# Chunked attention with a feed-forward block on one core: 64-token chunks as four 64x64 TensorE tiles

## The chip, the cores and the metric

The kernel runs on one NeuronCore of one Trainium2 chip. Five engines work from queues of their own: TensorE (PE, matrix products, with weight loads listed as PEld), VectorE (DVE), ScalarE (ACT), GpSimd (POOL) and SyncE (SP, which issues nearly all the transfers). [...] The metric is the device time of one execution in microseconds (us); lower is better.

## What is computed

Six groups of 512 tokens go through a decayed linear attention with 8 heads of 64 columns, then through an RMS norm and a gated feed-forward block (512 to 1536 to 512). Cut to what matters:

```python
# attention, per batch (4) and head (8), 768 tokens, blocks of 64
Dmask = lam ** (i - j) where i >= j else 0          # 64 x 64
intra = (q_b @ k_b.T * Dmask) @ v_b
inter = (q_b * lam ** (pos + 1)) @ kv_state
out_b = intra + inter
kv_state = lam ** 64 * kv_state + (k_b * lam ** (63 - pos)).T @ v_b
# block, per token
xn = x / sqrt(mean(x * x) + 1e-6) * rms_g
y = (silu(xn @ w_gate) * (xn @ w_val)) @ w_out
```

The block size of the recurrence is free: the same output comes from blocks of 128 with lam ** 128. The products have to be good to float32. The feed-forward splits its operands into a high and a low 16-bit part and adds three products; the attention uses float32 operands as they are.

## The kernel before

**Tiling.** The 3072 tokens are six groups m of 512, each with four chunks of 128 tokens (GC = 4); six chunks make one sequence, after which the state starts again. The 8 heads are four pairs p; a pair fills the 128 partitions, one head in each half. Pair(m, p) is one unit of attention, and there are 24 of them. The feed-forward is cut into 72 units u = (m, f), f being one of 12 blocks of 128 hidden columns. Units of the first 24 places are "classical" (line 761: gate and value products, 128x512); the later ones use a scheme with seven half-size products (line 948). Lines 780 to 782 are the output product.

**One pair of attention** has these steps.

- scores (line 507): keys by queries, 8 matmuls, one for each chunk and head. A head has 64 rows of the array (its partitions) and all 128 columns, so two matmuls, one for each head, can be under way at once. A row of the trace shows this form as 64*128.
- decay_k (ACT, line 517), decay_a (DVE, line 527, from PSUM, 128x512 twice), decay_q (POOL, line 531).
- state_sums (line 540): decayed keys by values, 128 tokens deep, 64x64 out; form 128*64. The last chunk of a sequence needs none, so there are 8 or 6 matmuls.
- states (DVE, lines 553 and 555): the running state, one 64-column operation for each chunk, straight from PSUM.
- mix_chunks (line 572): values by decayed scores, form 128*64, 8 matmuls of 128 columns. mix_states (line 583): state by queries, form 64*64, 8 matmuls or 6 (the first chunk of a sequence has no state), added to the same bank.
- keep_output (ACT, line 595) and keep_squares (ACT, line 606), both from PSUM.

A float32 matmul runs as two passes, so the trace counts 16 where the program has 8.

**Order.** Nothing is scheduled on the chip: each engine runs its instructions in program order. A class Plan takes all steps with an engine, a cost, a due time, what they read and write and which buffers they need, and lists them in the order of a list scheduler; a table SHIFTS moves the due times of single steps. TURN is what it adds when PE goes from one kind of matmul to another. Where it sees PE idle early on, busy() (line 142) puts in matmuls of the identity whose result is not read. The first group's attention and norm run alone (the ramp, until the first row of line 761); the other 19 pairs lie between the products of the feed-forward units.

**Banks.** PSUM has eight banks of 128x512 float32: ps0, ps1 (scores, and the products of even late units), pg, pv (classical products, products of odd late units, and a pair's state sums and output), po0 to po3 (output products).

Of the kernel before, what the change touches and what calls it, by code (L numbers as in the profile page):

```python
# [9 lines left out]
F32 = mybir.dt.float32  # L10
# [7 lines left out]
P = 128  # L18
# [5 lines left out]
def retention_swiglu_kernel(  # L24
# [28 lines left out]
    heads = [slice(j * D, (j + 1) * D) for j in range(2)]  # L53
# [21 lines left out]
    lam_b, lam_p, gcol = cs[:, :H], cs[:, H : H + NP], cs[:, H + NP :]  # L75
# [60 lines left out]
    SLOTS = GC + 1  # L136

    def busy(n, bank=3):

        ps = ps_out.tile([P, DM], F32, tag=f"po{bank}", name=f"unread{bank}")  # L140
        for _ in range(n):
            nc.tensor.matmul(ps[:, :P], ident, ident, start=True, stop=True)

    state = const.tile([P, NP, SLOTS, D], F32, name="state")


    mask = const.tile([P, H, P], F32, name="mask")

    pw = const.tile([P, NP, P], F32, name="pw")

    def powers(p, part):
        if part < 2:
            h = 2 * p + part
            nc.vector.tensor_tensor_scan(
                mask[:, h, :], lam_b[:, h : h + 1].broadcast_to([P, P]), ident, 0.0,
                ALU.mult, ALU.add,
            )
        else:
            nc.vector.tensor_tensor_scan(  # L159
                pw[:, p, :], lam_p[:, p : p + 1].broadcast_to([P, P]), zeros, 1.0,  # L160
                ALU.mult, ALU.add,
            )
# [48 lines left out]
    zeros = wg[:, NF - 1, 1].bitcast(F32)[:, :P]  # L211
    nc.scalar.mul(zeros, ones, 0.0)
# [275 lines left out]
    class Pair:  # L488
# [3 lines left out]
        def __init__(self, m, p):  # L492
            self.m, self.p = m, p
            self.odd = m == 0 and p % 2 or m == 1 and p == 0
# [3 lines left out]
        def scores(self, chunks=range(GC)):  # L498
            m, p = self.m, self.p
            if 0 in chunks:  # L500
                self.pa = [
                    ps_att.tile([P, GC, P], F32, tag=f"ps{j}", name=f"pa_{m}_{p}_{j}")
                    for j in range(2)
                ]
            for c in chunks:
                for j, r in enumerate(heads):
                    nc.tensor.matmul(  # L507
                        self.pa[j][:, c, :], self.kT[r, c, :], self.qT[r, c, :],
                        start=True, stop=True,
                    )  # L510

        def decay_k(self, half=None):
            for j, r in enumerate(heads):
                if half in (0, 1) and j != half:
                    continue
                last = mask[:, 2 * self.p + j, P - 1 : P]
                nc.scalar.mul(self.k[:, :, r], self.k[:, :, r], last)

        def decay_a(self, part=None):
            p = self.p  # L520
            if not part:
                self.a = att.tile([P, 2, GC, P], F32, tag="a", name=f"a_{self.m}_{p}", bufs=2)
            for j in range(2):
                if part in (None, j):
                    h = 2 * p + j
                    decay = mask[:, h : h + 1, :].broadcast_to([P, GC, P])
                    nc.vector.tensor_mul(self.a[:, j], self.pa[j], decay)

        def decay_q(self, eng=nc.gpsimd):
            p = self.p  # L530
            eng.tensor_mul(self.qT, self.qT, pw[:, p : p + 1, :].broadcast_to([P, GC, P]))  # L531

        def state_sums(self):
            m, p = self.m, self.p
            pool, tag = (ps_out, "po0") if self.odd else (ps_gv, "pg")
            self.pst = pool.tile([P, GC, P], F32, tag=tag, name=f"pst_{m}_{p}")[:, :, :D]
            for c in range(GC):
# [1349 lines left out]
```

## Time and profile before

| what | value |
|---|---|
| device time, median of 3 | 655.14 us (653.78 to 655.64) |
| span of the profiled execution, first to last instruction | 652.3 us |
| median less that span | 2.8 us |
| PE busy | 642.5 us, 98% of the span |
| DVE busy | 433.9 us, 67% |
| ACT busy | 334.8 us, 51% |
| POOL busy | 149.4 us, 23% |
| transfers | 51.13 MB, mean 78 GB/s |

For the profiled execution the span is the only time on the page, so the sum below is made against 652.3 us, and the 2.8 us are carried along. A busy PE is not PE at its best: the trace counts a matmul from its start to its modelled end, and several overlap. The length of a group is therefore read from its start to the start of the group behind it.

### The profile page before, as it was taken

Reading aid. Unit: us, or ns where it says so; the run is one execution under the profiler, and the core shown is the slowest. Engines: PE = TensorE matmul, PEld = TensorE weight load, DVE = VectorE, ACT = ScalarE, POOL = GpSimd, SP = SyncE. Lnnn points to the kernel's source line nnn. Section 1 sums busy time; section 2 is a strip of 40 time slices with the busy share of each in tenths; the row PEclk is TensorE's granted clock in tenths of the full one; section 3 lists DMA queues with packets and bytes.
Section 4 is the critical chain, followed back from the end, with each engine's and each line's share of the span. In section 5 each row is a group of like instructions: output and inputs, shape, how many; then the busy total and the mean of one; then the engine's idle time right before and its main releaser. Section 6 shows DMA issues by size and latency. Waiting matters only on the chain.

```text
span 652.3 us, 12342 instructions
## 1 busy us (share of the span) xinstructions
PE 642.5 (98%) x5016; PEld 442.0 (68%) x5016; DVE 433.9 (67%) x836; ACT 334.8 (51%) x676; POOL 149.4 (23%) x133
## 2 busy tenths in 40 slices
PE   7999999999999999999999999999999999999997
PEld 6846564755656645777777777777777777777774
DVE  6798897968997659656589634587543488544334
ACT  2876876756774444444545533335444334533332
POOL 2213040003477654354703011002010101100000
PEclk9999999999999999999999999999999999999999
DMA  8956653411002400101300311100220000000001
GB/s 328 327 211 221 238 191 133 169 58 65 1 24 91 146 2 1 65 4 63 130 2 2 130 65 65 66 1 1 97 99 1 2 2 1 33 33 1 2 1 65
DMA packets 14314, 51.13 MB, mean 78 GB/s; under 512 B 1713, under 2 KB 1969, under 8 KB 12849
## 3 DMA queue, kind: packets, MB, share of 16 engines
q1 hardware_dynamic: 13968, 50.21, 21.5%
q8 instruction: 39, 0.64, 0.4%
q10 hardware_dynamic: 288, 0.14, 0.1%
q14 instruction: 19, 0.15, 0.1%
HBM read 44.05 MB, written 6.29 MB: 77 GB/s over the span
## 4 chain that ended last, share of the span: by engine, by line
PE 95%; DVE 3%; DMA 1%; issue 0%; POOL 0%; ACT 0%; DVEq 0%; ACTq 0%
PE pa L948 20%; PE pb L948 15%; PE acc L780 10%; PE acc L782 10%; PE acc L781 10%; PE pg L761 9%; PE pv L761 9%; PE pa L507 4%; PE po L572 3%; PE po L583 3%; PE pst L540 2%; PE pss L628 1%; DMA cs<-in_consts_dram 1%; DVE xn L714 0%; DVE pw L159 0%
## 5 line engine op out<-in xcount | busy, mean ns | idle before, releaser
L996 ACT COPY tx<-pa 128x256 f32<-128x256 f32 x144 | 53.6, 372 | 136.6 <-PE pa L948 134.9
L782 PE MATMUL acc<-wo,hh 128*128 128x512 f16 (+1 forms) x288 | 110.2, 383 | 0.0
L781 PE MATMUL acc<-wo,hh 128*128 128x512 f16 (+1 forms) x288 | 110.1, 382 | 0.0
L1000 DVE TENSOR_TENSOR tx<-pb,tx 128x256 f32<-128x256 f32 x96 | 40.8, 425 | 65.3 <-PE pb L948 59.9
L780 PE MATMUL acc<-wo,hh 128*128 128x512 f16 x216 | 81.8, 379 | 0.0
L1004 DVE TENSOR_TENSOR sg<-pb,tx 128x256 f32<-128x256 f32 x48 | 20.4, 425 | 78.5 <-ACT tx L996 76.1
L948 PEld LDWEIGHTS <-wo 128*128 128x128 f16 x576 | 54.9, 98 | 23.2 <-issue 1.7
L761 PE MATMUL pg<-x,wg 128*128 128x512 f16 x288 | 67.7, 379 | 1.3 <-DVE wg L467 0.7
L761 PE MATMUL pv<-x,wv 128*128 128x512 f16 x288 | 67.5, 379 | 0.0
L948 PEld LDWEIGHTS <-wg 128*128 128x128 f16 x576 | 56.3, 98 | 16.2 <-issue 0.3
L1041 ACT CAST hh<-sg 128x512 f16<-128x512 f32 (+2 forms) x73 | 44.7, 612 | 35.6 <-DVE sg L1016 15.4
L948 PEld LDWEIGHTS <-wv 128*128 128x128 f16 x576 | 56.3, 98 | 8.3 <-issue 0.2
L531 POOL TENSOR_TENSOR qkv<-qkv,pw 128x512 f32<-128x512 f32 x24 | 32.2, 1342 | 77.3 <-PE pa L507 71.1
L761 PEld LDWEIGHTS <-wg 128*128 128x128 f16 x288 | 26.8, 98 | 33.8 <-issue 2.4
L761 PEld LDWEIGHTS <-wv 128*128 128x128 f16 x288 | 27.1, 98 | 32.9 <-issue 1.2
L1052 DVE TENSOR_TENSOR hh<-sg,hh 128x512 f16<-128x512 f32 x53 | 39.2, 739 | 7.8 <-ACT hh L1041 3.5
L1016 DVE SCALAR_TENSOR_TENSOR sg<-tx,cv,sg 128x512 f32<-128x512 f32 (+1 forms) x49 | 39.3, 803 | 5.6 <-ACT sg L1008 0.7
L948 PE MATMUL pa<-tx,wo 128*128 128x256 f16 x288 | 39.4, 273 | 0.0
L948 PE MATMUL pb<-tx,wo 128*128 128x256 f16 x288 | 39.3, 273 | 0.0
L948 PE MATMUL pa<-x,wv 128*128 128x256 f16 x288 | 39.3, 273 | 0.0
L948 PE MATMUL pa<-x,wg 128*128 128x256 f16 x288 | 39.3, 273 | 0.0
L948 PE MATMUL pb<-x,wv 128*128 128x256 f16 x288 | 39.3, 273 | 0.0
(186 smaller groups left out, 1152.1 us busy)
## 6 DMA issues: line engine op xcount, KB each, us to landing
qkv<-in_qkv_dram SPq DMA_DIRECT2D x48, 512.0 KB, 4.8
raw_gv<-in_weights_dram SPq DMA_DIRECT2D x11, 1024.0 KB, 6.3
raw_o<-in_weights_dram SPq DMA_DIRECT2D x12, 512.0 KB, 4.1
out_dram<-o SPq DMA_DIRECT2D x23, 256.0 KB, 2.1
partial<-in_weights_dram SPq DMA_DIRECT2D x2, 512.0 KB, 11.1
out_dram<-o ACTq DMA_DIRECT2D x1, 128.0 KB, 2.4
out_dram<-o SPq DMA_DIRECT2D x1, 128.0 KB, 2.4
cs<-in_consts_dram ACTq DMA_DIRECT2D x1, 8.0 KB, 4.7
```

Of the source, the lines that this page charges most:

```text
L507: nc.tensor.matmul(self.pa[j][:, c, :], self.kT[r, c, :], self.qT[r, c, :], start=True, stop=True,)
L531: eng.tensor_mul(self.qT, self.qT, pw[:, p : p + 1, :].broadcast_to([P, GC, P]))
L761: nc.tensor.matmul(ps, w[:, kk, :], x[:, kk, :], start=i == kk == 0, stop=i == 2 and kk == NK - 1,)
L780: nc.tensor.matmul(acc[:, cols], hl[:, ts_], oh, start=first, stop=False, skip_group_check=True)
L781: nc.tensor.matmul(acc[:, cols], hh[:, ts_], ol, start=False, stop=False, skip_group_check=True)
L782: nc.tensor.matmul(acc[:, cols], hh[:, ts_], oh, start=False, stop=last, skip_group_check=True)
L948: nc.tensor.matmul(ps, w(ow, k), x(ox, k), start=first and i == k == 0, stop=i == 2 and k == 1, skip_group_check=True,)
L996: nc.scalar.copy(self.kept[:, i], self.pa)
L1000: nc.vector.tensor_add(self.val[:, half], self.pb, self.kept[:, i])
L1016: nc.vector.scalar_tensor_tensor(sg, self.val[:, half], cv[:, self.f : self.f + 1], sg, ALU.mult, ALU.mult)
L1041: nc.scalar.copy(self.hh[:, half], self.sg[:, half])
L1052: nc.vector.tensor_sub(self.hl, self.sg, hh)
```

## The change

Attention is cut into chunks of 64 tokens, two of which (o = 0, 1) share the old chunk of 128. All four products of a pair become 64x64x64, 16 matmuls each (14 mix_states where a sequence starts), and they go round the four quarters of the array (row half r, column half out). For that the host lays keys and queries out with the two heads swapped in every odd chunk, and the output is kept in two tiles, one for each o.

```diff
 def scores(self, chunks=range(GC)):
...
     for c in chunks:
-        for j, r in enumerate(heads):
-            nc.tensor.matmul(
-                self.pa[j][:, c, :], self.kT[r, c, :], self.qT[r, c, :],
-                start=True, stop=True,
-            )
+        for o, keys in enumerate(lanes):
+            for s, r in enumerate(lanes):
+                nc.tensor.matmul(
+                    self.pa[s][keys, c, :], self.kT[r, c, lanes[o]], self.qT[r, c, lanes[o]],
+                    start=True, stop=True,
+                )
...
+def state_sums(self):
+    for c in range(GC):
+        for o, r in enumerate(lanes):
+            for h, out in enumerate(lanes):
+                nc.tensor.matmul(
+                    self.pst[o][out, c, :], self.k[r, c, lanes[h ^ o]], self.v[r, c, lanes[h]],
...
+def mix_chunks(self):
...
+                    nc.tensor.matmul(
+                        self.po[o][out, c, :], self.v[r, c, lanes[h]], self.a[r, h ^ o, c, :],
...
+def mix_states(self):
...
+                    for h, out in enumerate(lanes):
+                        r = lanes[h ^ o]
+                        if o:
+                            st = self.turned[r, c, :]
+                        else:
+                            st = self.n[r, c, :]
```

The state is no longer taken chunk by chunk from PSUM. Two sums of 64 tokens are first joined to one of 128 (decay_sums on ACT, whole_sums on DVE); a chain of 64-column operations, one for each 128 tokens, gives the state at each old chunk (chain); one wide operation gives the state in its middle (middle); and since odd chunks have the heads swapped, ACT copies that across the partition halves (turn). mix_states waits for all of it.

```diff
+def decay_sums(self):
+    nc.scalar.mul(self.turned, self.pst[0], pw[:, self.p, 0, D - 1 : D])
+def whole_sums(self):
+    nc.vector.tensor_add(self.n[:, 1:], self.turned, self.pst[1])
+def chain(self, chunks):
...
+            nc.vector.scalar_tensor_tensor(
+                to, self.n[:, c], both[:, self.p : self.p + 1], self.n[:, c + 1],
+                ALU.mult, ALU.add,
+            )
+def middle(self):
+    nc.vector.scalar_tensor_tensor(
+        self.mid, self.n[:, :GC], pw[:, self.p, 0, D - 1 : D], self.pst[0],
+        ALU.mult, ALU.add,
+    )
+def turn(self):
+    for s, r in enumerate(lanes):
+        nc.scalar.copy(self.turned[r], self.mid[lanes[1 - s]])
```

The rest: decay_a works on 128x256 twice; POOL starts the chain (begin, a 128x64 copy or memset); keep_output copies two tiles; keep_squares squares the copy in SBUF and no longer the bank. A pair's output and state sums now share two banks, from mix_chunks until keep_output has read them: ps0 and ps1 for most of groups 1 and 2, pg and pv for later groups. The scans of powers are 64 columns wide. busy() issues wider matmuls, and the threshold from which it fills is 0.4 instead of 0.8.

In the planner, mix_chunks and state_sums now stand together ahead of the chain, and mix_states alone behind it. It has a fourth kind of PE step, new loads for transfers and for a few operations, and new shifts (here two entries of some 640):

```diff
-    step("PE", 0.5, at, q.state_sums, r=[f"q{n}:k", f"q{n}:v"], w=[f"pst{n}", "turn:pst"],
+    step("PE", 0.47, at + 0.01, q.state_sums, r=[f"q{n}:k", f"q{n}:v"], w=[f"po{n}_0", f"po{n}_1"])
+    step("POOL", 0.25, at - 1, q.begin, r=[f"state{q.p}"], w=[f"a{n}:n"])
+    step("ACT", 0.4, at - 1, q.decay_sums, r=[f"pw{q.p}", f"po{n}_0"], w=[f"a{n}:T"])
+    step("DVE", 0.42, at - 1, q.whole_sums, r=[f"a{n}:T", f"po{n}_1"], w=[f"a{n}:w"])
...
-    step("LD", 2.8, -9, load_next, w=w, new=[(name, "in")], lasts=1.8)
+    step("LD", 2.6, -9, load_next, w=w, new=[(name, "in")], lasts=4.0 if p and m > 2 else 2.8)
...
-        62: 0.65, 63: 0.95, 67: 1.15, 80: 1.35, 81: 2.05, 93: -0.95, 101: 1.6, 102: -2.2, 106: 3.3,
+        57: -0.1, 58: 2.25, 59: -3.7, 65: 2.45, 67: 5.3, 75: 4.35, 85: 4.3, 89: 1, 93: -1.3, 95:
```

What that does to the instructions shows at pair (1, 2) and its neighbours, early in the feed-forward. In the rows, po is a pair's output (in the changed kernel with its state sums), pa its scores, acc the output product, pg and pv the gate and value products. On PE before, the scores of one pair, the mixing of another and its state part follow each other without a break:

```order
L507 MATMUL pa_2_1_647<-qkv_2_583 128x128
L572 MATMUL po_1_663<-a_1_612,qkv_1_473 64x128 x8
L583 MATMUL po_1_663<-qkv_1_473,state 64x128 x6
L761 LDWEIGHTS wg
L761 MATMUL pg_2_688<-x_240,wg 128x512
```

On PE in the changed kernel, the state sums of the pair end and an output product follows:

```order
L554 MATMUL po_2_0_1049<-qkv_2_866 64x64 x2
L554 MATMUL po_2_1_1050<-qkv_2_866 64x64 x2
L820 MATMUL acc_0_3_1011<-wo_1047,hl_1_944 128x512
L821 MATMUL acc_0_3_1011<-wo_1047,hh_1_894 128x512
L822 MATMUL acc_0_3_1011<-wo_1047,hh_1_894 128x512
L820 MATMUL acc_0_2_914<-wo_1047,hl_1_944 128x512
```

Mixing and state part have come apart: 12 output matmuls and 4 of pg stand between line 554 and line 623 of this pair.

On DVE before, the state of the pair is three small operations between weight conversion and gating:

```order
L227 TENSOR_SCALAR wg<-wg 128x512
L555 SCALAR_TENSOR_TENSOR state<-state,pw,pst_2_741 128x64
L553 COPY state<-pst_2_741 128x64
L555 SCALAR_TENSOR_TENSOR state<-state,pw,pst_2_741 128x64
L1029 SCALAR_TENSOR_TENSOR sg_2_727<-pv_2_717,cg,sg_2_727 128x512
```

On DVE in the changed kernel, at the same pair:

```order
L260 TENSOR_TENSOR wo_1047<-wg,wo_1047 128x512
L260 TENSOR_TENSOR wo_1086<-wg,wo_1086 128x512
L572 TENSOR_TENSOR a_2_1015<-a_2_1015,po_2_1_1050 128x256
L580 SCALAR_TENSOR_TENSOR a_2_1015<-a_2_1015,both 128x64
L578 MEMSET a_2_1015 128x64
L586 SCALAR_TENSOR_TENSOR a_2_1015<-a_2_1015,pw,po_2_0_1049 128x256
L580 SCALAR_TENSOR_TENSOR state<-a_2_1015,both 128x64
```

Two wide operations (lines 572 and 586) have joined the narrow ones, and they read a tile that ACT writes first. On ACT in the changed kernel, between the first and the last step of that chain:

```order
L569 ACTIVATE a_2_1015<-po_2_0_1049,pw 128x256
L531 ACTIVATE qkv_3_988<-qkv_3_988,mask 128x4x64 x2
L228 ACTIVATE wg<-raw_o_971 128x512
L593 COPY a_2_1015<-a_2_1015 64x256 x2
L1062 ACTIVATE sg_3_1136<-pg_3_1020,cg 128x512
```

Three rows of other work stand on ACT between decay_sums (line 569) and turn (line 593), for which PE waits.

## Rows read from the trace of the kernel before

**Rows 1.** The page: engine, busy us, share of the span, instructions; the granted clock.

```profile
PE 642.5 (98%) x5016; PEld 442.0 (68%) x5016; DVE 433.9 (67%) x836; ACT 334.8 (51%) x676; POOL 149.4 (23%) x133
...
PEclk9999999999999999999999999999999999999999
```

**Rows 2.** Busy time in four stretches: stretch and length, engines' busy time, clock, DMA.

```profile
0.00:34.00 34.00, 29.89 (x372) 25.86 (x373) 24.29 (x62) 18.97 (x38) 9.52 (x16) 1.00 0.90 329
34.00:100.00 66.00, 64.60 (x423) 38.08 (x422) 60.37 (x116) 51.03 (x95) 14.40 (x11) 1.00 0.57 206
100.00:600.00 500.00, 499.80 (x3875) 344.00 (x3874) 328.47 (x621) 246.57 (x505) 125.50 (x107) 1.00 0.15 51
600.00:652.30 52.30, 48.23 (x351) 34.09 (x349) 20.72 (x39) 18.23 (x40) 0.00 (x0) 0.99 0.06 21
```

**Rows 3.** Who PE waited for, total us, times, longest: the first of seven rows.

```profile
PE pa L507 <- DVE a L527: 1.6, 1, 1.6
```

**Rows 4.** PE in order of time at two pairs: start, us, engine, line, form, count.

```profile
44.59 0.57 PE L540 MATMUL pst<-qkv 128*64 128x64 f32 x12
45.09 1.90 PE L761 MATMUL pv<-x,wv 128*128 128x512 f16 x8
46.83 0.17 PE L445 MATMUL pn<-ssq,ones_b 128*128 128x2 bf16 x1
...
47.81 1.16 PE L507 MATMUL pa<-qkv 64*128 64x128 f32 x16
48.91 1.09 PE L572 MATMUL po<-a,qkv 128*64 128x128 f32 x16
49.93 0.87 PE L583 MATMUL po<-qkv,state 64*64 64x128 f32 x12
50.73 1.47 PE L761 MATMUL pg<-x,wg 128*128 128x512 f16 x6
```

**Rows 5.** PE in order of time in the ramp, two groups of one form together.

```profile
21.73 1.09 PE L572 MATMUL po<-a,qkv 128*64 128x128 f32 x16
22.66 0.63 PE L540 MATMUL pst<-qkv 128*64 128x64 f32 x16
23.22 2.05 PE L628 MATMUL pss<-ones,sq 128*128 128x128 f32 x16
25.20 0.87 PE L583 MATMUL po<-qkv,state 64*64 64x128 f32 x12
```

**Rows 6.** Passes of line 540 begun by 22.708, by 22.712 and by 22.718.

```profile
22.66 0.23 PE L540 MATMUL pst<-qkv 128*64 128x64 f32 x2
...
22.66 0.28 PE L540 MATMUL pst<-qkv 128*64 128x64 f32 x3
...
22.66 0.28 PE L540 MATMUL pst<-qkv 128*64 128x64 f32 x4
```

**Rows 7.** Groups by line: out<-in, shapes, count, then busy us and mean ns.

```profile
L996 ACT COPY tx<-pa 128x256 f32<-128x256 f32 x144 | 53.6, 372 | 136.6 <-PE pa L948 134.9
...
L1000 DVE TENSOR_TENSOR tx<-pb,tx 128x256 f32<-128x256 f32 x96 | 40.8, 425 | 65.3 <-PE pb L948 59.9
...
L527 DVE TENSOR_TENSOR a<-pa,mask 128x512 f32<-128x512 f32 x48 | 31.1, 683 | 9.2 <-PE pa L507 6.8 <-PE po L572 2.3
...
L555 DVE SCALAR_TENSOR_TENSOR state<-state,pw,pst 128x64 f32<-128x64 f32 x64 | 17.8, 279 | 2.9 <-PE pst L540 1.2
```

**Rows 8.** ACT in order of time behind the last row of Rows 5.

```profile
26.12 0.59 ACT L595 COPY x<-po 128x512 f32<-128x512 f32 x1 [0.65 <-PE po L583]
```

**Rows 9.** PE at the end of the ramp, with what ended its waits.

```profile
33.59 0.62 PE L761 MATMUL pg<-x,wg 128*128 128x512 f16 x2
...
37.23 1.90 PE L761 MATMUL pg<-x,wg 128*128 128x512 f16 x8 [0.67 <-DVE wg L467]
```

**Rows 10.** PE in order of time: two output matmuls of a classical unit.

```profile
63.41 0.39 PE L781 MATMUL acc<-wo,hh 128*128 128x512 f32 x1
63.64 0.40 PE L782 MATMUL acc<-wo,hh 128*128 128x512 f32 x1
```

More of the change, by code (lines that the diff above doesn't have):

```diff
@@ L512, in decay_k @@
[L512 to L527, printed above, removed]
@@ L1083, in retention_swiglu_kernel @@
         }
[L1085 to L1089 removed]
+        SINGLE = {"row_sums", "spread", "quick", "largest_of_all"}
+        TILED = {"scores", "state_sums", "mix_chunks", "mix_states"}
+        TURN = (
+            (0.0, 0.1, 0.2, 0.08), (0.03, 0.0, 0.12, 0.1), (0.03, 0.2, 0.0, 0.1), (0.13, 0.13, 0.13, 0.0)
+        )
         def __init__(self):
@@ L1440, in pair_sums @@
         n = f"{q.m}_{q.p}"
-        step("PE", 0.5, at, q.state_sums, r=[f"q{n}:k", f"q{n}:v"], w=[f"pst{n}", "turn:pst"],
-             new=[(f"pst{n}", "po0" if q.odd else "pg")])
-        for i in range(2):
-            step("DVE", 0.58, at - 1, q.states, range(2 * i, 2 * i + 2), r=[f"pst{n}", f"pw{q.p}"], w=[f"state{q.p}"])
+        step("PE", 0.5, at, q.mix_chunks, r=[f"q{n}:v", f"a{n}:0", f"a{n}:1"], w=[f"po{n}_0", f"po{n}_1", "turn:po"],
+             new=[(f"po{n}_{o}", q.banks[o]) for o in range(2)]
+             + [(f"x{q.m}", f"xs{SLOT_OF[q.m]}")] * (q.p == 0))
+        step("PE", 0.47, at + 0.01, q.state_sums, r=[f"q{n}:k", f"q{n}:v"], w=[f"po{n}_0", f"po{n}_1"])
+        step("POOL", 0.25, at - 1, q.begin, r=[f"state{q.p}"], w=[f"a{n}:n"])
+        step("ACT", 0.4, at - 1, q.decay_sums, r=[f"pw{q.p}", f"po{n}_0"], w=[f"a{n}:T"])
+        step("DVE", 0.42, at - 1, q.whole_sums, r=[f"a{n}:T", f"po{n}_1"], w=[f"a{n}:w"])
+        step("DVE", 0.9 - 0.2 * (q.m % 3 < 2), at - 1, q.chain, range(GC - 1), r=[f"a{n}:w"], w=[f"a{n}:n"])
+        step("DVE", 0.42, at - 1, q.middle, r=[f"a{n}:n", f"po{n}_0"], w=[f"a{n}:M"])
+        step("ACT", 0.7, at - 1, q.turn, r=[f"a{n}:M"], w=[f"a{n}:T"])
+        if (q.m + 1) * GC % SEQ_CH and q.m < NG - 1:
+            step("DVE", 0.28, at - 0.9, q.chain, [GC - 1], r=[f"a{n}:n", f"a{n}:w"], w=[f"state{q.p}"])
     def pair_mix(q, at):
@@ L1448, in pair_mix @@
         m, p = q.m, q.p
[L1449 to L1455 removed]
+        step("PE", 0.47, at, q.mix_states, r=[f"q{n}:q", f"a{n}:n", f"a{n}:T"], w=[f"po{n}_0", f"po{n}_1"])
+        step("ACT", 0.67, at - 1, q.keep_output, r=[f"po{n}_0", f"po{n}_1"], w=[f"x{m}:h{p}", f"x{m}:l{p}"])
+        step("ACT", 0.59, at - 1, q.keep_squares, r=[f"x{m}:h{p}"], w=[f"s{n}", f"rows{m}"],
              new=[(f"s{n}", "t" if p else "sq")])
@@ L1799, in retention_swiglu_kernel @@
                     norm_steps(m + 1, u, 0.2)
-        for i, by in SHIFTS.items():
-            eng, cost, at, *rest = plan.steps[i]
-            plan.steps[i] = (eng, cost, at + by, *rest)
+        for i, (eng, cost, at, *rest) in enumerate(plan.steps):
+            plan.steps[i] = (eng, cost, round(at + SHIFTS.get(i, 0), 4), *rest)
         order = plan.run()
@@ L1810, in retention_swiglu_kernel @@
                 idle = t - now
-                if spare_bank and idle > 0.8:
-                    busy(int((idle - 0.2) / 0.4))
+                if spare_bank and idle > 0.4:
+                    busy(int((idle - 0.1) / 0.28))
                 now = t + cost
```

228 lines of the change are left out of this document (114 added, 114 removed), and 103 rows, old and new, of the table SHIFTS.

## The prediction

> **What bounds the kernel now.** [...] A share of the whole span can hide a stage with another limit, so the second view cuts the span in four [rows 2]: up to 34 us the ramp, where PE has gaps (29.9 of 34) and the transfers are at 0.90; then a stretch where PE is full (64.6 of 66) but DVE is nearly so too (60.4 of 66); then 500 us in which PE is busy 499.8 and DVE two thirds; then the end. The third view says what PE waited for: seven rows with 5.6 us in all, the longest 1.6, and all but 0.2 of it ahead of 41 us [rows 3]. So from 41 us on what PE issues is the time, and a microsecond taken out of its queue is a microsecond of span, as long as nobody becomes late.
>
> **What attention costs on PE.** Read from start to start, one pair early in the feed-forward takes 1.10 us for the scores, 1.02 for mix_chunks, 0.80 for mix_states (12 passes) and its neighbour 0.50 for state_sums (12 passes) [rows 4]. In each the passes go two at a time, so 16 passes are 8 rounds. How much of that is rounds and how much is the change of form? mix_chunks followed by state_sums, which has the same form, takes 0.93 [rows 5]; followed by another form it took 1.02 [rows 4]; leaving a form costs 0.09. state_sums entered without a change takes 0.56 for 8 rounds [rows 5]; less 0.09 for leaving, a round of 64 columns is 0.058 us. The 6 rounds behind a change took 0.50 [rows 4]; less 0.35 and 0.09, entering has 0.06 more to pay for weights that nothing covers. A round of 128 columns is (0.93 - 0.06) / 8 = 0.109.
>
> **Before, outside the ramp.** The program's PE order has 19 pairs there, in 39 stretches of attention between other matmuls. 19 x (1.10 + 1.02 + 0.80 + 0.50) = 65.0. Eight of the pairs have 8 rounds of mix_states and not 6: + 8 x 0.22 = 1.8; four have 8 of state_sums: + 0.5. Each stretch makes the work ahead of it leave its form: 39 x 0.09 = 3.5. In seven, state_sums and mix_chunks stand together and save a change: - 7 x 0.15 = 1.0. Sum 69.8 us.
>
> **After.** Every product of a pair becomes 16 matmuls of 64 columns, 32 passes, on four quarters of the array. No row of before has four quarters at work. If all four run together, a group is 8 rounds of 0.058 = 0.47 us. For that speaks that every two quarters that share anything already run side by side here: two column halves on the same rows (lines 540 and 572), two row halves on the same columns (line 507), and the diagonal (line 583), each at the pace of one matmul. So I take 0.47. The lower bound is the same, since a round can't be shorter than one quarter's own 64 columns; the upper bound is that no more passes begin in a microsecond than do with two quarters, 16 in 0.47 us, so 0.94. In the changed order the same part has 77 groups (19 x 4 and a mix_states that came out of the ramp) in 48 stretches: 77 x 0.47 = 36.2, and 48 x (0.09 + 0.06 + 0.09) = 11.5. Sum 47.7. The form is now changed more often, but only into one form, so a run of groups pays once. **Difference: 69.8 - 47.7 = 22.1 us off PE's queue.**
>
> Does anything keep the passes apart? In one group of state_sums two passes have begun by 22.708, three by 22.712 and four by 22.718 [rows 6]: the third and the fourth, which are on different halves, start at most 10 ns apart. Four such starts, 40 ns, fit in a round of 58. [...]
>
> **The new chain, and what covers it.** mix_states used to wait for 64-column operations on DVE. It now waits for decay_sums (ACT, 128x256 from PSUM: as line 996, 0.37), whole_sums (DVE, 128x256: as line 1000, 0.43), two or three links (as line 555, 0.28 each), middle (0.43) and two copies of turn (0.37 each) [rows 7]: 0.37 + 0.43 + 0.84 + 0.43 + 0.74 = 2.8 us, and four hand-overs. One from PE to ACT is 0.05 (line 583 ends at 25.20 + 0.87, line 595 starts at 26.12) [rows 5, 8]. With 0.1 for each of the others about 3.2. Against it stands what PE does between line 554 and line 623 of the pair. At pair (1, 2) that is 12 output matmuls of 0.23 [rows 10] and 4 of the gate product of 0.22, as 8 of line 761 took 45.09 to 46.83 [rows 4]: 3.6, and 0.2 for the two changes of form. That is the shortest cover outside the ramp, and five pairs have about it; the others have 4 to 8 us. So the chain is hidden by half a microsecond where it is shortest, if ACT and DVE come at once. They don't always: behind decay_sums ACT has two decay_k and a weight lift, and DVE is 91% busy there [rows 2]. If all 19 pairs were hidden, the cost is 0; if the five short ones each lose 1.4 us, it is 7. I take 1, nearer to the lower end because the work that stands between on ACT is shorter than DVE's part of the chain.
>
> Also on the queues, and hidden. DVE per pair: decay_a goes from 2 x 0.68 to 2 x 0.43, the states from about 0.9 to 0.43 + 0.84 + 0.43; net + 0.3, 7 us in all on an engine with 218 us to spare. ACT per pair: + 0.37 + 0.74 and 0.15 for the second copy of keep_output, 30 us on 335. POOL gets a small copy. PSUM banks of a pair are held longer, some 4 us, over work that uses the other banks; if a product wants them too early, PE waits, and that is in the 7 us. SP's queue keeps its transfers.
>
> **The ramp.** It ends with the first row of line 761 at 33.59, and PE isn't full until 37.2, when a weight part on DVE arrives [rows 9]. PE has less to do, DVE about as much, the chain to mix_states is longer, and the new fills stand for 42 matmuls of 128 columns, 15 before. PE isn't the limit, so its saving counts for nothing here. I take 0, with 3 us either way: three is what comes back of 37.2 - 33.6 if the weight part comes early, and what 27 more fills cost at 0.1 us apiece.
>
> **Sum.** 652.3 - 22.1 + 1 + 0 = 631.2 us of span; with the 2.8 us that lie between span and median, 634.
>
> **Rivals.**
> (1) Four quarters don't run together. Then a round of four takes up to 0.117 and a group 0.94: 77 x 0.47 = 36 us come back, and the time is 670. The point from which it decides is a round of 0.058 + 22.1 / (77 x 8) = 0.094: above that the kernel is slower. This is also the case in which the change doesn't do what it says. Against it: [rows 6], and the forms that run side by side today. For it: no row has four. Chance 0.07.
> (2) The chain takes PE's place. If ACT and DVE reach its steps a microsecond late at each of the 19 pairs (both have work of 0.7 us and more ahead in their queues), 19 x 0.9 = 17 us come back and the time is about 650. Against it: from 100 us on ACT is half idle and DVE a third [rows 2]. Chance 0.07.
> (3) The ramp gains more than I allow, since its whole order is new: 626 or less. Chance 0.06.
>
> **How the numbers follow.** Forecast 634 with 0.80. Its bounds: 22.1 off, ramp - 3 and no waits give 630; ramp + 3 and 7 us of waits give 643; three or four more on the low side for an error of 0.005 us in a round (3 us over 616 rounds). Range 626 to 644. About 0.3%, 2 us, is what a measurement of this kernel can tell from no change. Faster by more than that: forecast, rival 3 and nearly all of rival 2, 0.91; within it 0.02; slower 0.07, rival 1.
>
> **What would show it.** In the changed trace: groups of 32 passes that follow each other 0.47 us apart inside a stretch; PE busy 98% or more from 41 us on with no row of waits over 2 us behind 100 us; line 623 not waiting for ACT's line 593 by more than a few tenths; the first row of line 801 (761 before) between 31 and 36 us. [...]

## The result

| what | before | after |
|---|---|---|
| device time, median | 655.32 us (4 runs, 653.78 to 655.64) | 646.13 us (4 runs, 643.41 to 647.64) |
| ratio, 95% interval | | 0.986 (0.9827 to 0.9894) |
| span of the profiled execution | 652.3 us | 643.0 us |
| attention matmuls, start to start, behind the 36th product | 66.7 us | 45.0 us |
| start of the 36th product of line 761 / 801 (last of pg, unit 1) | 43.06 us | 47.85 us |
| from there to the end of the span | 609.2 us | 595.15 us |

The change gains 9.2 us; the forecast was 21, and the time lies 2.1 us above the range. The two last rows say where to look. The 36th product is the same work in both kernels and lies behind the ramp. It is the last of the twelve in each of these rows, before and after:

```profile
40.69 2.75 PE L761 MATMUL pg<-x,wg 128*128 128x512 f16 x12
```

```profile
45.46 2.76 PE L801 MATMUL pg<-x,wg 128*128 128x512 f16 x12
```

The stretch behind it became shorter, but by 14.1 us, and the stretch ahead of it longer by 4.8.

The page of the changed kernel: span, busy times, the clock in 40 slices, and PE's instruction transfers (packets, MB, share of the DMA engines).

```profile
span 643.0 us, 15756 instructions
...
PE 624.5 (97%) x6612; PEld 420.0 (65%) x6612; DVE 438.1 (68%) x884; ACT 363.0 (56%) x772; POOL 158.7 (25%) x158
...
PEclk9999999999999999999999999999999999999999
...
q8 instruction: 52, 0.85, 0.5%
```

PE's share fell from 98% to 97% [rows 1], its idle time rose from 9.8 to 18.5 us, and the clock is full. In the same four stretches as [rows 2] (columns: stretch, length, busy PE, PEld, DVE, ACT, POOL with instructions, clock, DMA share, GB/s):

```profile
0.00:34.00 34.00, 27.57 (x653) 19.42 (x654) 19.89 (x66) 20.97 (x47) 9.28 (x21) 1.00 0.85 310
34.00:100.00 66.00, 64.12 (x654) 37.23 (x653) 58.51 (x118) 55.10 (x107) 16.30 (x14) 1.00 0.53 193
100.00:600.00 500.00, 493.83 (x5032) 336.32 (x5031) 343.05 (x670) 273.45 (x588) 133.11 (x124) 1.00 0.16 54
600.00:643.00 43.00, 38.93 (x279) 27.00 (x276) 16.61 (x31) 13.43 (x32) 0.00 (x0) 0.99 0.07 25
```

In the long third stretch PE, busy 499.8 of 500 us before, now stands for 6.2; ahead of 34 us it is busy 27.6 for 29.9. What PE waited for (total us, times, longest), in place of the seven rows that [rows 3] stands for:

```profile
PE pa L524 <- issue: 2.6, 1, 2.6
PE po L623 <- DVE a L586: 2.2, 3, 1.0
PE po L605 <- issue: 2.0, 1, 2.0
PE po L623 <- ACT a L593: 1.8, 4, 0.5
...
PE pv L801 <- DVE sg L1069: 1.3, 1, 1.3
PE pb L988 <- DVE tx L1040: 0.8, 2, 0.5
PE pg L801 <- ACT x L759: 0.8, 1, 0.8
PE pg L801 <- DVE wg L477: 0.5, 1, 0.5
```

Before it was 5.6 us in all and 0.2 behind 41 us. Now there are two kinds: two long stops with "issue" as releaser, both in the ramp, and waits for DVE and ACT behind it.

**The groups came out as forecast.** PE's timeline in the ramp (start, us, line, form, count):

```profile
17.98 0.69 PE L605 MATMUL po<-a,qkv 64*64 64x64 f32 x32
18.49 0.65 PE L554 MATMUL po<-qkv 64*64 64x64 f32 x32
18.96 0.68 PE L524 MATMUL pa<-qkv 64*64 64x64 f32 x29
```

18.49 to 18.96 is 0.47 for 32 passes on four quarters. mix_chunks takes 0.51, the step into the next product included. Summed from the start of each matmul to the start of the next, over all attention matmuls behind the 36th product, attention takes 66.7 us before and 45.0 after. Of the 45.0 us 1.4 are waits inside groups of line 623, and one group of scores (0.6) now lies ahead of the mark. Like for like that is 66.7 - (45.0 + 0.6 - 1.4) = 22.5 us saved; eight more stretches that make other work leave its form cost 8 x 0.09 = 0.7. The forecast's 22.1 is 21.8 here.

**The waits behind the ramp** are the distances from start to start that exceed the usual ones. At line 623 they are 4.2 us, in three pairs at 216, 226 and 237 us and one at 317. At other products they are 3.9: line 801 for line 477 at 62 us (0.8) and for line 1069 at 107 (2.0 with its neighbours), line 988 for line 1040 at 323 and 537 (1.1). Together 8.1 where the sum had 1. 21.8 - 8.1 = 13.7; the table has 14.1, less the 0.6 of the scores that moved 13.5. The ramp's 4.8 less the same 0.6 is 4.2. So 643.0 = 652.3 - 13.5 + 4.2.

### The profile page after: what moved, and what is told of

It reads as the page before. It is cut to its first block, busy times and chain, and to the rows that moved or that the text cites. A ratio compares the mean times of both kernels' runs of the same rounds, so it can differ in the third digit from the quotient of the medians.

```text
span 643.0 us, 15756 instructions
## 1 busy us (share of the span) xinstructions
PE 624.5 (97%) x6612; PEld 420.0 (65%) x6612; DVE 438.1 (68%) x884; ACT 363.0 (56%) x772; POOL 158.7 (25%) x158
## 4 chain that ended last, share of the span: by engine, by line
PE 84%; DVE 10%; ACT 3%; issue 2%; POOL 0%; DVEq 0%; ACTq 0%; POOLq 0%
PE pa L988 18%; PE pb L988 14%; PE acc L820 9%; PE acc L822 8%; PE acc L821 8%; PE pv L801 8%; PE pg L801 8%; PE po L605 2%; PE pa L524 2%; PE po L623 2%; PE unread L141 2%; PE po L554 2%; DVE a L580 2%; DVE w L240 1%; PE pss L668 1%
## 5 line engine op out<-in xcount | busy, mean ns | idle before, releaser
L822 PE MATMUL acc<-wo,hh 128*128 128x512 f16 (+2 forms) x288 | 110.2, 383 | 0.0
L821 PE MATMUL acc<-wo,hh 128*128 128x512 f16 (+2 forms) x288 | 110.1, 382 | 0.0
L801 PE MATMUL pv<-x,wv 128*128 128x512 f16 x288 | 69.4, 379 | 1.8 <-DVE sg L1069 1.3
L1092 DVE TENSOR_TENSOR hh<-sg,hh 128x512 f16<-128x512 f32 x53 | 37.6, 709 | 11.7 <-ACT hh L1081 11.5
L1048 ACT ACTIVATE sg<-sg,cg 128x256 f32<-128x256 f32 x48 | 24.4, 508 | 31.6 <-DVE sg L1044 31.5
## 6 DMA issues: line engine op xcount, KB each, us to landing
partial<-in_weights_dram SPq DMA_DIRECT2D x2, 512.0 KB, 11.6
```

Of the source, the lines that this page charges most:

```text
L801: nc.tensor.matmul(ps, w[:, kk, :], x[:, kk, :], start=i == kk == 0, stop=i == 2 and kk == NK - 1,)
L821: nc.tensor.matmul(acc[:, cols], hh[:, ts_], ol, start=False, stop=False, skip_group_check=True)
L822: nc.tensor.matmul(acc[:, cols], hh[:, ts_], oh, start=False, stop=last, skip_group_check=True)
L1048: nc.scalar.activation(self.sg[:, half], self.sg[:, half] if t else self.pa, AF.Silu, scale=cg[:, self.f, 0:1],)
L1092: nc.vector.tensor_sub(self.hl, self.sg, hh)
```

## The links: a row that did not carry over

The chain of the pair at 216 us on DVE and POOL (start, us, engine, line, count), and the wait of PE behind it:

```profile
213.23 2.21 DVE L580 SCALAR_TENSOR_TENSOR a<-a,both 128x64 f32<-128x64 f32 x3
215.47 0.48 DVE L586 SCALAR_TENSOR_TENSOR a<-a,pw,po 128x256 f32<-128x256 f32 x1
```

```profile
212.10 1.83 POOL L288 TENSOR_TENSOR wo<-rest_h,rest_l 128x512 f16<-128x512 f32 x1 [1.76 <-DVE rest_h L283]
213.88 1.16 POOL L920 TENSOR_TENSOR r<-wg 128x512 f32<-128x512 f16 x1
```

```profile
216.10 0.33 PE L623 MATMUL po<-qkv,a 64*64 64x64 f32 x4 [0.98 <-DVE a L586]
216.91 0.68 PE L623 MATMUL po<-qkv,a 64*64 64x64 f32 x28 [0.48 <-ACT a L593]
```

Three links take 2.21 us; the sum had 3 x 0.28. The second ends at 215.12, just as POOL's line 920 ends at 215.04. Over the whole kernel, 48 links that write the chain (ns: shortest, median, longest):

```profile
L580 DVE SCALAR_TENSOR_TENSOR a<-a,both x48: 275/285/1326, 11.9 to 509.0; 128x64 f32<-128x64 f32 x48
```

The price 0.28 came from line 555 [rows 7]. That operation reads one operand from PSUM. Beside a running POOL operation it keeps its time, as these rows of the kernel before show:

```profile
191.53 0.91 DVE L555 SCALAR_TENSOR_TENSOR state<-state,pw,pst 128x64 f32<-128x64 f32 x3
```

```profile
191.40 1.23 POOL L917 TENSOR_TENSOR wo<-ws,wo 128x512 f16<-128x512 f32 x1 [1.14 <-ACT wo L913]
```

The new link has both operands in SBUF. In the changed kernel 18 of line 580's 64 operations take over 0.3 us, and each of the 18 ends 0.08 or 0.09 us behind the end of a POOL operation. Theory A: such an operation waits until POOL's has ended. Rival B: the links are late because of the work ahead of them. The experiment gives the link a PSUM operand again:

```diff
 def whole_sums(self):
-    nc.vector.tensor_add(self.n[:, 1:], self.turned, self.pst[1])
+    nc.vector.tensor_add(self.pst[1], self.turned, self.pst[1])
 def chain(self, chunks):
...
-    elif not self.starts(c):
+    else:
...
-        to, self.n[:, c], both[:, self.p : self.p + 1], self.n[:, c + 1],
+        to, self.n[:, c], both[:, self.p : self.p + 1], self.pst[1][:, c],
```

> Edit: whole_sums writes its result back into the PSUM bank of the second sum, and each link reads it there, so that a link has one operand in PSUM and one in SBUF, as line 555 had in the kernel before. The order of all engines stays; a sequence's first link is now an operation where it was none (8 more on DVE). Theory A (in the changed kernel a link takes 0.28 us, but 0.6 to 1.3 where a POOL operation runs beside it, because both of its operands lie in SBUF): links fall to 0.28 everywhere, also beside POOL; the six waits of line 623 for lines 586 and 593 at 215 to 237 us shrink from 3.3 us to under 1; the time falls by 3 to 5 us, to about 642. Rival B (the links are late because of what stands ahead of them on DVE and ACT): links may get shorter, but the waits of line 623 stay above 2.5 us and the time within 1 us of the changed kernel's 646.

Measured: 642.24 us (641.94 to 642.63), ratio to before 0.9798 (0.9769 to 0.9826); 3.9 us under the changed kernel. The links again, the same pair, and POOL beside it:

```profile
L580 DVE SCALAR_TENSOR_TENSOR a<-a,both,po x64: 249/281/283, 10.7 to 506.3; 128x64 f32<-128x64 f32 x64
```

```profile
214.51 0.91 DVE L580 SCALAR_TENSOR_TENSOR a<-a,both,po 128x64 f32<-128x64 f32 x3
```

```profile
213.38 1.82 POOL L288 TENSOR_TENSOR wo<-rest_h,rest_l 128x512 f16<-128x512 f32 x1 [1.97 <-DVE rest_h L283]
215.16 1.15 POOL L920 TENSOR_TENSOR r<-wg 128x512 f32<-128x512 f16 x1
```

All links lie between 0.25 and 0.28, POOL or no POOL, and the three waits at 216 to 237 us are gone. What is left of line 623's waits behind the ramp is one of 0.3 us. Theory A holds, with 1.33 us at worst for a link of 0.28, and the number of links even rose by sixteen.

Is it the links alone? At 107 us PE waits 1.3 for line 1069, and no pair is near. DVE there, ahead of that line:

```profile
101.71 2.06 DVE L240 SCALAR_TENSOR_TENSOR w<-raw_gv,w 128x1024 int32<-128x1024 int32 x1
103.69 1.38 DVE L237 TENSOR_SCALAR wv<-wv 128x512 int32<-128x512 int32 x1
...
107.78 0.74 DVE L1069 SCALAR_TENSOR_TENSOR sg<-pv,cg,sg 128x512 f32<-128x512 f32 x1
```

On POOL three sums of weights (line 920) run from 98.99 to 104.78. The run moves them, and the DVE operation that reads them, behind 159 us, with the links from PSUM. (move takes steps of the plan by their numbers and puts them behind the step named last.)

```diff
         order = plan.run()
+        move((730, 800, 801, 802), 651)   # line 920 three times, line 935; behind line 288
```

> Links from PSUM, and the three sums of weights that POOL runs from 99 to 105 us in the changed kernel (line 920, beside them line 240 on DVE takes 2.06 us for 1.22 and line 237 1.38 for 0.42) stand behind the first halves of POOL (line 288, about 160 us), with the DVE operation that reads them. Theory A (a POOL operation holds up any DVE operation with all operands in SBUF, not the links alone): lines 237 and 240 take 0.42 and 1.23 again, the wait of line 801 for line 1069 at 107 us (1.3) goes, and so do 0.4 us of slower products beside it: 640.5 against 642.2 of links_psum. Rival (DVE is late there for the amount of its work): the wait stays. If the sums are needed sooner than they now come, a new wait appears behind 165 us.

```profile
101.22 1.22 DVE L240 SCALAR_TENSOR_TENSOR w<-raw_gv,w 128x1024 int32<-128x1024 int32 x1
102.36 0.42 DVE L237 TENSOR_SCALAR wv<-wv 128x512 int32<-128x512 int32 x1
...
105.69 0.75 DVE L1069 SCALAR_TENSOR_TENSOR sg<-pv,cg,sg 128x512 f32<-128x512 f32 x1
```

Line 240 takes 1.22 for 2.06 and line 237, which has one input only, 0.42 for 1.38; line 1069 no longer holds PE there. But the sums are needed where they now are, and a new wait appears:

```profile
174.80 0.16 PE L331 MATMUL pc<-ones_b,sq_w 128*128 128x1 bf16 x1 [1.33 <-DVE e L462]
...
178.95 1.24 PE L801 MATMUL pv<-x,wv 128*128 128x512 f16 x5 [0.66 <-DVE sg L1069]
```

645.51 us (642.47 to 646.12), 3.3 us over 642.24: one wait of 1.3 us went, two of 1.3 and 0.7 came. These are the waits of the profiled execution, the fastest of the four (642.47); what more the three others lost, at 645.17 and above, no trace shows. So the slowing beside POOL is not the links' alone; the place of POOL's work was not free to choose.

What does the chain cost in all? In the next run begin, links, middle and turn are left out, and mix_states reads whole_sums. What it computes is no longer the attention; it bounds the cost:

```diff
-                        if o:
-                            st = self.turned[r, c, :]
-                        else:
-                            st = self.n[r, c, :]
+                        st = self.n[r, c + 1, :]
```

> Left out: the start of the chain on POOL, the links (lines 578 and 580), middle (586) and turn (593); mix_states reads the sums of whole_sums in place of the states, so its waits end with line 572. Per pair 0.28 to 0.84 + 0.48 us of DVE and 0.81 of ACT are gone; the order of all the rest stays. It bounds what the new chain costs in all, in waits of PE and by the room that it takes on DVE and ACT. Theory A (of the chain it is the links beside POOL that cost, and the remaining waits at 62, 107, 323 and 537 us are other work's): 642, as with links that read PSUM. Rival B (the chain costs as such, its other steps delay the weights and the gate behind them on DVE and ACT): 638 or less, the waits of line 801 for line 1069 (1.3 us at 107) and of line 988 for line 1040 (0.8) go too, and the ramp's pg without a break starts at 41 instead of 43.

637.48 us (637.35 to 638.88), ratio 0.9747 (0.9731 to 0.9764), 8.7 us under the changed kernel. B's number, but not all of B's reasons: the wait for line 1069 stayed (1.3), and that for line 1040 fell to 0.3. In the profiled execution the 36th product starts at 45.66 instead of 47.85, and from there to the end it is 590.0 us, against 591.8 with links from PSUM and 595.15 in the changed kernel. So of the 7.3 us between these two profiled executions 3.4 are the links beside POOL, 1.8 the room that the rest takes behind the ramp, and 2.2 lie in the ramp. Those 2.2 are hardly the chain's own: line 701's product pr starts at 31.36 instead of 33.34, because a long stop of PE ahead of it, which the next section takes up, is absent, and from pr to the 36th product it takes 14.30 us instead of 14.51.

## The ramp: PE runs out of instructions

Of the 4.8 us that the 36th product comes later, 2.8 arise ahead of line 701's product pr, which spreads the norm; in the kernel before it started at 30.51:

```profile
30.51 1.16 PE L661 MATMUL pr<-ident,y 128*128 128x128 f32 x8
```

The second long stop of PE in the changed kernel, in the middle of mix_chunks of pair (1, 0), and pr behind it:

```profile
29.46 0.16 PE L455 MATMUL pn<-ssq,ones_b 128*128 128x2 bf16 x1
29.56 0.56 PE L605 MATMUL po<-a,qkv 64*64 64x64 f32 x21
32.17 0.39 PE L605 MATMUL po<-a,qkv 64*64 64x64 f32 x10 [2.05 <-issue]
...
33.34 1.06 PE L701 MATMUL pr<-ident,y 128*128 128x128 f32 x8
...
37.85 1.46 PE L801 MATMUL pg<-x,wg 128*128 128x512 f16 x6 [0.77 <-ACT x L759]
```

Nothing that the profile knows is waited for. Counting PE's records (matmuls, weight loads and the rows of its sequencer) from the start, the stop is at number 1217; the first one (12.70 to 15.29, in scores of pair (0, 2)) is at 449. They are 768 = 3 x 256 apart. The instruction transfers of PE, 52 packets of 16 KB for 13,284 records and 39 for 10,097 before, carry about 256 each. The packet behind the first stop starts at 12.84 and takes 0.95, PE goes on at 15.29; behind the second, 29.82, 0.94 and 32.17. PE had entered the block that it then used up at 9.6 and 23.8 us; until the packet for the next one began it took 3.3 and 6.0 us, with the loads at a DMA share of 0.9 and more.

Theory C: PE's instructions come in blocks of 256, one ahead, and behind the loads. A product of a pair is now 64 records (32 passes and their weight loads) in 0.5 us, where it was 32 in 1 us, so PE reaches the end of a block too early. The rival: the stops belong to the work itself. Four runs decide. The first takes out the fills, so that other work stands at the ends of the blocks:

```diff
-                if spare_bank and idle > 0.4:
+                if False:
```

> Edit: busy() puts in no matmuls of the identity at all; all else stays. Two things are read. (1) Fills hold up the first scores: they start at 6.88 us behind six fill passes in the changed kernel, at 5.28 in the kernel before. Without fills they start at about 5.3. [...] (2) Theory C (PE stands still because its next 256 instructions have not been brought in): the two stops inside a group, 12.70 to 15.29 and 30.12 to 32.17 us, are at PE's 512th and 1280th instruction, counted with 63 that the trace lacks. With about 13 and 50 instructions of fills fewer ahead of them the stops, if any, come that many instructions later in the program. Rival D (the stops belong to what is computed there, scores of pair (0, 2) and mix_chunks of pair (1, 0)): they stay at the same matmul.

650.40 us (649.40 to 651.89), slower by 4.3. Stops inside a group are now at 13.31, 19.43, 27.71 and 37.22 us, in scores, scores, mix_states and state_sums, at records 449, 705, 961 and 1217: every one a whole number of blocks from the others. The 63 that the expectation adds to them is an estimate, 512 less 449; the runs show the distances. The work there is other work. The numbers are those of the changed kernel, the matmuls are later ones, as many as fills are missing. The fills do pay. Without them PE begins at half pace: mix_chunks takes 1.04 us at 10.26 and 0.60 at 24.99, in the changed kernel 0.52 at 8.82 already. pr comes at 38.46, 5.1 us later. Behind 32 us the granted clock, 1.00 until then, falls (the third column from the end), and the first eight products of line 801, at 43.08, take 0.42 us apiece and not 0.22:

```profile
32.00:40.00 8.00, 6.92 (x132) 5.99 (x124) 3.28 (x9) 6.49 (x16) 2.43 (x3) 0.79 0.81 307
40.00:48.00 8.00, 5.08 (x13) 1.72 (x12) 7.90 (x16) 6.91 (x15) 1.68 (x1) 0.64 0.37 132
```

The second lets PE of the kernel before run through more instructions in a place where it has time, and the third occupies it as long with few:

```diff
+    def short(n=112, bank=3):   # behind the second fill
...
+            nc.tensor.matmul(two[i % 2][out, :16], ident[r, out], ident[r, :16], start=True, stop=True)
```

```diff
+    def short(n=2, bank=3):     # in the same place
...
+                ps, ident, ident[:, None, :].broadcast_to([P, GC, P]), start=True, stop=True,
```

> The kernel before, with 112 small matmuls of the identity (64x64 by 16 columns, float32, not read) behind its second fill at 6.9 us, where PE waits until 9.8 anyway: some 448 more instructions on PE in a place without work. Theory C (PE's instructions come in blocks of 256, and the next block but one is asked for when a block is finished, 3 us and more ahead of its arrival while the loads run): PE reaches its 512th instruction near 10 us instead of 21, its block arrives at about 13, PE stops there inside a run of equal matmuls for 1 to 3 us, at an index which with the same 63 is a multiple of 256, and the time is 656.5 to 658.5. Rival D (the number of instructions doesn't matter): no stop, and the time as of the next kernel or shorter, 655 to 656.

> The kernel before, with two wide matmuls of the identity (128x128 by 512 columns, float32, not read, about 3.4 us) in the same place: PE is occupied at least as long as by the small ones, with 8 instructions instead of 448. Both theories: the scores behind it start some 0.5 to 1 us late, no stop inside a group, 655 to 656.5. It is what the kernel with the small ones is held against.

before_wide: 654.96 us (ratio 1.0013, 1.0000 to 1.0026), no stop; the two matmuls took 1.9 us, not 3.4. before_many: 662.85 us (661.53 to 664.33), ratio 1.013 (1.0109 to 1.0152). Its PE:

```profile
8.01 2.97 PE L151 MATMUL short<-ident 64*64 64x16 f32 x187
14.64 1.25 PE L151 MATMUL short<-ident 64*64 64x16 f32 x37 [3.67 <-issue]
```

The stop is at record 449 again, inside 112 equal matmuls that wait for nothing, 3.67 us long. The small matmuls took more than I gave them (4.2 us without the stop, 2.3 more than the wide ones). Behind the stop the granted clock was lower as well, 0.70 from 16 to 24 us where it was 1.00 in before_wide, and the state sums, scores and mix_chunks there took 4.96 us for 2.84. So of the 8 us lost the stop itself is 3.7 and the slower matmuls behind it 2.1. In a place where the wide matmuls cost nothing, instructions alone make PE stand still.

The fourth kind holds loads back. SP issues loads from 24.6 to 28 us, ahead of the packet at 29.82; a small transfer that waits for the norm's y (31 us) was put ahead of them:

```diff
+            late = const.tile([P, GC], F32, name="late")
+            nc.sync.dma_start(late, self.y)
...
+        move((14, 15, 16), 147)                  # two blocks of weights, one of keys and queries
```

> Edit: the transfers of the third gate and value block, of an output block and of keys and queries of pair (1, 1), which SP issues from 24.6 to 28.0 us, stand behind a 2 KB transfer that waits for the norm's y (31.1 us). PE, DVE, ACT and POOL keep program and order. Theory C (PE's instructions are fetched by transfers of 16 KB that stand behind the loads: the one at 29.82 us starts 6 us after PE reached the block of 256 before it): with the loads gone from 24.6 to 31 us the fetch starts before 27 us, mix_chunks of pair (1, 0) runs in one piece of 0.5 us, the product pr starts at 31.3 instead of 33.34, and the time falls by up to 2 us to about 644. Rival D (PE stands still there for another reason): the stop of 2.0 us stays, and the time is the same or, by the later loads, up to 2 us longer.

646.50 us (645.87 to 646.83). The packet started at 27.29, the stop at 30 us was gone, pr came at 31.42 and the first gate product at 36.27 (37.85). And then PE stood for 2.8 us: ACT waited for the output block that had been held too. In the next version the block stands behind the held ones, and PE waits 5.5 us for it:

> The changed kernel with two of the three transfers of hold_loads held (gate and value block 2, keys and queries of pair (1, 1); needed at 43 and 45 us), while the output block that ACT reads at 37.7 keeps its place. Theory C, that the second stop is the block of instructions behind those loads: no stop at 30 us, pr at 31.4, the gate's first product at 36.2, no wait of 2.8 us for line 473 as in hold_loads, the value product's second part at 41 to 42 instead of 43.0, and the time 644 to 645 (646.1). Rival F (the ramp is bound by something that both kernels share): 646.

650.84 us (650.23 to 651.06). With the block ahead of them:

> As hold_two, but the output block that ACT reads at 37.7 us is now issued ahead of the held transfers (in hold_two it had slipped behind them, landed at 42.4 and held ACT and PE for 5.5 us). Held: gate and value block 2 and keys and queries of pair (1, 1). Theory C with a price (the second stop of PE puts off pr, and all behind it, by 1.9 us): no stop at 30 us, pr at 31.4 instead of 33.34, gate's first product at 36.2 to 36.5, the 36th product of line 801 at 46 instead of 47.85, and the time 644 to 645 (646.1). Rival F (behind pr the ramp waits for DVE and the weights, which gain nothing): the 36th product at 47.5 or later, 646.

643.88 us (642.94 to 645.00), ratio 0.9832 (0.9816 to 0.9849), 2.2 under the changed kernel, whose own runs spread over 4 us. The profiled execution had a longer first stop (3.14 for 2.60) and behind it a granted clock of 0.79 from 16 to 24 us (1.00 in the changed kernel). pn, the small product just ahead of mix_chunks, came 2.0 us later, so the later steps are best read from pn on:

```profile
31.51 0.16 PE L455 MATMUL pn<-ssq,ones_b 128*128 128x2 bf16 x1
31.60 0.69 PE L605 MATMUL po<-a,qkv 64*64 64x64 f32 x32
...
33.25 1.08 PE L704 MATMUL pr<-ident,y 128*128 128x128 f32 x8
```

pn to pr is 1.7 us instead of 3.9, pn to the 36th product 16.6 instead of 18.4. So the second stop costs about 2 us of ramp, and from the 36th product to the end both kernels take the same (595.1). Theory C holds: the longer stops at the ends of blocks took 2.0 to 3.7 us while loads ran.

Could the order have avoided it? Four runs changed it.

```diff
+        move((167, 169, 168), 148)                 # mix_chunks, state_sums of (1, 0) behind pr
+        move((171, 172, 173, 174, 176), 160)       # its chain and mix_states behind the low parts of x
```

> Edit: in the ramp the spreading of the norm (line 701, pr) stands ahead of mix_chunks and state_sums of pair (1, 0) on PE, and the chain of that pair (lines 572 to 593 and its mix_states) behind the low parts of x (line 762). Theory E (the ramp is late by two things ahead of x: the stop of 2.05 us in front of pr, and 2.0 us of the chain of pair (1, 0) between xn and x on DVE): pr starts at 31.2 (33.34), xn at 32.3 (34.43), x on DVE follows xn at once and ends by 37.5 (42.0), the first product that runs without a break starts near 39 instead of 43.0, and the time falls by 3 to 4.5 us, to about 642. Rival F (the ramp is bound by the loads or by weights, which keep their time): the first row of line 801 stays above 37 us, and the time within 1 us of 646.

646.19 us (645.64 to 647.14): no gain. pr came at 31.34, but xn at 33.01 for 34.43, since weight parts stood ahead of it on DVE, and x ended at 39.5; mix_states then waited until 41.77 for the chain, and the 36th product started at 48.12. DVE is without a break from 31.3 to 42.1 there: what is moved in its queue comes due elsewhere. The next run moved the chain of (1, 0) out of the ramp, with links from PSUM:

```diff
+        move((171, 172, 173, 174, 175, 176, 177, 178), 392)   # late_chain: behind pv of unit 1
+        move((171, 172, 173, 174, 175), 392)                  # late_chain2
+        move((176, 177, 178), 186)
```

> Links from PSUM as in the run links_psum, the norm's spreading ahead of mix_chunks of pair (1, 0) as in pr_first, and the chain, the mix_states and the keeping of pair (1, 0) behind the first value product of unit 1 (about 48 us) instead of ahead of it: 1.4 us of DVE and a wait of PE at 41 leave the ramp. Theory G (the ramp ends when DVE has worked off what stands in its queue from 31 to 43 us, so only less work there helps): the value product's second part starts at 41.5 instead of 43, and the time is 1.5 to 2 us under links_psum, 640 to 641. Rival H (the ramp waits for ACT and the weights' loads, not for DVE): within 0.7 us of links_psum's 642.2.

> As late_chain (links from PSUM, the norm's spreading first, the chain of pair (1, 0) behind the first value product of unit 1), but mix_states of that pair behind state_sums of pair (1, 1), and without the seven fills of 5.4 us that stood at 51 us in late_chain, a result of the moved step's old time. Theory G (the ramp ends when DVE has worked off its queue): pv's second part by 43.0 or before, mix_states at 52 without a wait, the time 640 to 641. Rival H (the ramp waits for ACT and the weights' loads): 642 as with links_psum.

late_chain: 648.75 us, because of 5.4 us of fills that the moved step drew in at 51 us. late_chain2, without them: 643.61 us (642.27 to 644.20), no gain over links_psum (642.24). The 36th product started at 45.90 (48.89 with links from PSUM alone), as theory G has it, but PE then waited for DVE, 0.7 at 49.2, 1.0 at 53.3 and 0.6 at 64.2; at the 72nd product 0.4 us of the 3.0 were left. Rival H's number, by another way: DVE is the limit until some 65 us, not only until 43.

> Both edits of late_chain2 and late_wholes, links from PSUM. If the two gains add up: 639 to 640, which is 15 us under the kernel before and 6.5 under the changed kernel.

644.58 us (643.92 to 644.78): nothing adds up here. The last run takes the links from PSUM and the held loads of hold_two2 together:

> Links from PSUM and the held transfers of hold_two2 together. If both gains hold: 640 to 641, the best version so far (links_psum 642.2). If the stop's time comes back as a wait for DVE: 642.

641.45 us (640.85 to 641.86, 5 runs), ratio 0.9793 (0.9779 to 0.9807). That is the best version that computes the whole result, 4.7 us under the changed kernel, where the two gains alone were 3.9 and 2.2. Over links_psum the held loads gain 0.8 us, and the intervals of the two ratios overlap: that they add something to it is not shown.

## Why the prediction was wrong, step by step

- **PE is the bound from 41 us on: right before, only nearly right after.** From 41 us on PE was busy 99.3% and is busy 98.2%; from 100 to 600 us alone 6.2 us are missing, and a row of waits of 2.2 us stands there, which the prediction had named as a sign against itself.
- **A group of 32 passes takes 0.47, the difference is 22.1 us: right.** 0.47 measured, 21.8 like for like. Rival 1 is out.
- **Line 623 doesn't wait for ACT's line 593 by more than a few tenths: right** (0.5 at most, and only behind a late line 586). It waited for the DVE part of the chain instead.
- **"It now waits for decay_sums [...] two or three links (as line 555, 0.28 each)": the first step that failed.** The row was right and the operand was not: 0.28 is the price with a PSUM operand. Two SBUF operands made it 0.28 to 1.33. The rest of the step held. The five shortest covers, from the end of line 554 to line 623, are 3.5 to 3.8 us, at 70, 81, 216, 226 and 237 us, as estimated (3.8). At 70 and 81, with POOL idle beside the links, the chain took 3.05 and 2.84 us (3.2 in the sum), and nothing was lost. At the other three POOL works beside the links (sums of weights, and squares at 237), the chain took 5.3, 5.3 and 4.8, and PE lost 1.5, 1.3 and 1.0; a fourth pair, at 317, lost 0.4. That is 4.2 us for the "I take 1".
- **The waits were looked for at mix_states and the banks only; DVE had "218 us to spare".** Another 3.9 us arose at other products that wait for DVE: 2.0 of it at 107 us, shown by late_wholes to be lines 237 and 240 beside line 920. The rest (62, 323 and 537 us) was not taken apart. Both show that "ACT is half idle and DVE a third" [rows 2] says nothing of when.
- **"PE isn't the limit, so its saving counts for nothing here. I take 0, with 3 us either way": the second step that failed.** The ramp lost 4.2 us. PE became the limit by its instructions, which the sum did not count: the second stop costs about 2 us. The run without the chain gains as much there because the stop is absent in it; what the chain itself adds behind pr stays open, at 14.51 us from pr to the 36th product, 14.30 without the chain and 14.02 with links from PSUM. One link beside POOL stands there, 1.18 us at 38.46 (0.27 from PSUM). What the first stop of 2.6 us costs was not isolated, and no run took it away.
- **The sum of it.** 643.0 is 11.8 us above the forecast span of 631.2: 0.3 for the groups, 7.1 for waits behind the ramp and 4.2 for the ramp make 11.6.
- **First row of line 801 between 31 and 36 us: wrong,** 37.85.
- Rival 2 (the chain takes PE's place, 650) had the right kind of loss and a quarter of its size at the chain itself (4.2 of 17 us), and put it down to the queues where it was DVE's SBUF operands beside POOL.

The trace of the kernel before would have told the first one. Line 230, whose operands lie in SBUF too, on 128x512, with POOL's line 722 beside it (90.67 to 91.84) and without:

```profile
91.23 1.15 DVE L230 SCALAR_TENSOR_TENSOR wg<-raw_o,wg 128x512 int32<-128x512 int32 x1
...
98.41 0.69 DVE L230 SCALAR_TENSOR_TENSOR wv<-raw_o,wv 128x512 int32<-128x512 int32 x1
```

## What to carry to other kernels

Price an operation from a row with the same operands in the same memories: when a step moves from PSUM to SBUF, look for rows of that kind beside a busy POOL before pricing it (here 0.28 us became up to 1.33). Splitting matmuls into smaller tiles multiplied PE's instructions here, 32 records of a product to 64; in a stretch where transfers fill the DMA engines, count PE's instructions as well as its columns, and hold back loads that aren't due. When a work-saving change gives back half its gain, compare one late milestone in both kernels first: it tells the ramp's loss from the rest.

## Not expected of the hardware

- DVE with all operands in SBUF was held up beside a running POOL operation: 0.28 became up to 1.33 us (line 580), 0.42 became 1.38 (line 237, one input), 1.22 became 2.06 (line 240). With one operand in PSUM 64 links lay between 0.249 and 0.283.
- PE stood 0.5 to 3.7 us at the end of a block of 256 instructions while loads ran, always at record 449, 705, 961 or 1217, in the changed kernel, in its variants and in the kernel before with more instructions.
- Behind the first stop the granted clock fell in some runs. From 16 to 24 us it was 0.84 in the run with links from PSUM and 0.70 in before_many, means over these 8 us; in the changed kernel, with a stop in the same place, it was 1.00. The two runs, columns as above:

```profile
16.00:24.00 8.00, 8.00 (x234) 6.15 (x232) 5.24 (x21) 5.38 (x14) 0.98 (x4) 0.84 0.71 215
```

```profile
16.00:24.00 8.00, 8.00 (x96) 6.85 (x97) 4.69 (x18) 1.08 (x2) 1.57 (x2) 0.70 0.19 54
```
